# Windowed attention and a gated two-layer product on one core: w_out's load, batch 0's last copies and the global rows' store in other places

## The chip, the cores and the metric

The kernel runs on one core of one Trainium2 chip. The metric is device time in microseconds (us) of the whole program, from three runs; besides these, one execution was recorded by the hardware profiler. Engines: PE (TensorE), DVE (VectorE), ACT (ScalarE), POOL (GpSimd) and SP, which only issues transfers. POOL issues transfers too; those that change the type (from float32 to bfloat16) all go through POOL's queue (q0, "software_dynamic"), SP's through q1 ("hardware_dynamic").

## The reference

Attention with a window of 32 to each side and 8 global tokens that see and are seen by all, for 8 batches, 8 heads, 576 tokens, 64 dimensions; then a product with `w_in`, a Snake activation and a product with `w_out`:

```python
scores = scale * np.matmul(q, k.transpose(0, 1, 3, 2))
mask = np.abs(pos[:, None] - pos[None, :]) <= window
mask = mask | is_global[:, None] | is_global[None, :]
attn = softmax(np.where(mask, scores, -1e9))        # written out in the reference
x = np.matmul(attn, v).transpose(0, 2, 1, 3).reshape(B * S, H * D)   # 4608 x 512
h = x @ w_in                                        # 4608 x 2048
g = h + np.sin(alpha * h) ** 2 / (alpha + 1e-09)
out = g @ w_out                                     # 4608 x 512, float32
```

## The kernel before

**Stages.** The program is one hand-written order; each engine works off its instructions in the order in which they are written. `phase_a(b, b_moe)` is the attention of batch `b`, with the second product (`gemm2`) of an earlier batch put between its steps; `gemm1(b)` is `x @ w_in` and the activation. The sequence is attention 0, then for each b: gemm1(b), attention(b + 1). Heads go in four pairs `hp`. In a pair: `scores` (PE), exponential to `E` (ACT), mask (DVE), `denominators` (PE, with a matrix of ones), logarithm and inverse exponential (ACT), `numerators` (PE, E with the values VX), product with the inverse into `xT` (DVE). LC keeps the logarithms in SBUF for a later test; they get there by small SP transfers.

**gemm1** runs over 16 groups `nt` of 128 columns of `w_in`. Three PSUM tiles (zn, zr, zd) rotate: PE fills one, ACT takes the sine of it (`sb`), ACT or DVE squares it (`s`), DVE writes `H2` (`H` in the trace) and so frees the tile. **gemm2** is a generator over blocks of 128 tokens, 16 matmuls each into one of two tiles zo, then ACT copies the block to `osb` (three buffers) and SP stores it. `fill(n)` takes its next n matmuls; the tables FIRST, SECOND, NEAR, MIDST, PER_GROUP, GROUP_LATE and GROUP_LAST say how many at which place. Two batches make nine blocks; for the last two, five are left for batch 7.

**Transfers.** For each batch, POOL casts k, q and v to DRAM (`kd`, `qd`, `vd`); SP transposes kd and qd into SBUF (`kt`, `qt`, `turn_qk`), and DVE copies from there into KX and QX (`place`); SP loads vd into VX (`load_v`). Batch 0 has a way of its own: its tokens are loaded directly, transposed by PE, and copied from PSUM by ACT (into KD) and DVE (into QX); the second half of the heads (pairs 2 and 3) is `second_half`. w_in comes in four casts, the last two behind the wait `pace`, which is a copy of one element of kt by POOL to the tile `seen`, so that POOL's queue stands until kt has landed. The global tokens' values are gathered by SP from v into a part of H2 (`gather(v, gv)`), cast by POOL into VGb, and loaded by SP into VX (`load_vg`).

**Global rows.** The output rows of global tokens are computed apart (64 extra columns in batch 7's gemm1, `gemm2_globals` after everything else) and stored by an indirect transfer from POOL (the scatter) over the rows that were stored before. At the end `judge` and `judge_sums` test whether the fast path's assumptions hold; a branch on `verdict` goes to `general_path` if they don't, which it doesn't here.

Of the kernel before, what the change touches and what calls it, by code (L numbers as in the profile page):

```python
# [249 lines left out]
def kernel(  # L250
# [66 lines left out]
    seen = main.tile([1, 1], DT.bfloat16, name="seen")  # L317
# [21 lines left out]
    def cast_v(b):  # L339

        cast[b, "vd"] = dramp.tile([S, H, D], DT.bfloat16, name="vd")
        nc.gpsimd.dma_start(out=cast[b, "vd"][:], in_=v[b].rearrange("h s d -> s h d"))

    def turn_qk(b):

# [435 lines left out]
    def attention_first(beside):  # L781


        b = 0
        kx, qx, VXb = KD, QX[0], VD
        xT = xpool.tile([P, CT, SG], DT.bfloat16, name="xT")
        xTs[b] = xT
        Es, Rs, begun = {}, {}, set()
        ring = tc.alloc_tile_pool(name="ringp", bufs=2, space=PSUM)
        pair = {}  # L790

        def scores(hp, g):
# [12 lines left out]
            nc.vector.tensor_tensor(  # L805
                out=Eg, in0=Eg, in1=MASK[:, 4 * g : 4 * g + 4, :].rearrange("p i c -> p (i c)"),
                op=ALU.mult,
            )

        def nd(hp, key):  # L810


            t = (zn, zd)[key] if hp < NHP - 1 else (pair["zr"] if key else zd)
            return t[:].rearrange("p k (x c) -> p k x c", x=2)

        def products(hp, gs, keys=(0, 1)):


            E = Es[hp][:].rearrange("p i (x c) -> p i x c", x=2)
            for g in gs:  # L820
                for key in keys:
                    out_t = nd(hp, key)
                    for i in range(4 * g, 4 * g + 4):
                        s0 = begin(i)
                        a, z = max(s0, 0), min(s0 + 60, QLEN)
                        if z <= CUT + 4:
                            parts = [(0, a, z)]
                        elif a >= CUT:
                            parts = [(1, a, z)]
                        elif i % 2:  # L830
                            parts = [(0, a, CUT + 4), (1, CUT + 4, z)]
                        else:
                            parts = [(0, a, CUT), (1, CUT, z)]
                        for half, a, z in parts:
                            bank = (hp, key, half)
                            nc.tensor.matmul(
                                out=out_t[:, half, :, a - half * CUT : z - half * CUT],
                                lhsT=OB[:] if key else VXb[:, hp, i, :],
                                rhs=E[:, i, :, a - s0 : z - s0],
                                start=bank not in begun, stop=True, skip_group_check=True,  # L840
                            )
# [12 lines left out]
        def normalise(hp):  # L854
            nc.vector.tensor_tensor(
                out=xT[:, hp, 0:S].rearrange("p (k m c) -> p k m c", k=4, c=KT), in0=body(hp, 0),
                in1=Rs[hp][:], op=ALU.mult,
            )

        def idle(hp):  # L860
            if hp > 1:
                warm(zo[0], 1)

        for hp in range(NHP):
            Es[hp] = pairp.tile([P, NT12, WCOL], DT.bfloat16, name="E")
            for g in range(2):
                scores(hp, g)
                idle(hp)
            if hp:
                products(hp - 1, range(3), (1,))  # L870
            scores(hp, 2)
            idle(hp)
            if hp:
                products(hp - 1, range(3), (0,))
            if hp:
                inverse(hp - 1)
                sums(hp - 1, 1)
# [12 lines left out]
        sums(last, 0)  # L890
        normalise(last)

        beside(NHP)
        after.release()


    def attention(b, beside):
# [208 lines left out]
    def gemm1(b):  # L1106
# [23 lines left out]
        for nt in range(NT):  # L1130
# [33 lines left out]
        hr.release()  # L1164


    def gemm2(b):
        lo, hi = (0, 4) if b % 2 == 0 else (4, 9)
        for blk in range(lo, hi):
            ops = zo[(blk + b // 2) % 2]  # L1170
            for nt in range(NT):
                nc.tensor.matmul(  # L1172
                    out=ops[:], lhsT=H2[:, nt, blk * P : (blk + 1) * P], rhs=w_out[:, nt, :],
                    start=(nt == 0), stop=(nt == NT - 1),
                )
                yield True
            osb = osbp.tile([P, DM], DT.float32, name="osb")
            if b == B - 1 and blk == hi - 1:
                for e, copy in enumerate((nc.scalar.copy, nc.vector.tensor_copy)):
                    copy(out=osb[:, e * DM // 2 : (e + 1) * DM // 2], in_=ops[:, e * DM // 2 : (e + 1) * DM // 2])  # L1180
            else:
                nc.scalar.copy(out=osb[:], in_=ops[:])  # L1182

            c = blk * P
            while c < (blk + 1) * P:
                z = min((c // QTR + 1) * QTR, (blk + 1) * P)
                run, u = c // QTR, c % QTR
                t0 = (b // 2) * 2 * S + (run // 2) * HALF + run % 2 + 2 * u
                nc.sync.dma_start(
                    out=out[t0 : t0 + 2 * (z - c) - 1 : 2, :], in_=osb[c - blk * P : z - blk * P, :]  # L1190
                )
                c = z

    def gemm2_globals():

# [43 lines left out]
    def pace(src):  # L1239

        nc.gpsimd.tensor_copy(out=seen[:], in_=src)  # L1241

    def phase_a(b_att, b_moe):
        def beside(at):

            if b_moe is None:
                if at == 0:
                    second_half()
                    turn_qk(1)
                    pace(turned[1][1][0:1, 0:1])  # L1250
                    load_w_in((2, 3))
                    cast_v(1)
                    load_w_out()
                    gather(v, gv)
                if at == 2:
                    load_v(1)
# [24 lines left out]

    phase_a(0, None)
    for b in range(B):
        if b == 1:
            pace(turned[2][0][0:1, 0:1])
            cast_v(2)
# [8 lines left out]
        if b + 1 < B:  # L1295
# [19 lines left out]
    with tc.If(sure < P):  # L1315
        general_path(tc, q, k, v, global_idx, out, w_in, w_out, alphaT, recipT)


# [28 lines left out]
```

## Time and profile before

| | |
|---|---|
| median of 3 runs | 382.67 us (382.43 to 382.87) |
| the profiled execution | 384.38 us, span 382.7 us, mean granted PE clock 0.97 |
| busy: PE, weight loads, DVE, ACT, POOL | 323.6, 206.1, 275.5, 288.9, 55.1 us |
| q0, POOL's queue | 18.52 MB, 39.9% of 16 DMA engines |
| q1, SP's queue | 23.97 MB, 30.2% |

Shares are of the span. A row of a timeline is start, duration, engine, line, operation, what is written <- what is read, count, and in brackets the idle time of the engine before it with what ended that. A row with "SPq" or "POOLq" is the issuing of a transfer and not its landing. "xN" rows are merged: the duration is from the first to the last of N.

### The profile page before, as it was taken

The page shows a single profiled execution, that of the slowest core. Times are in us where ns is not written, and L with a number is a line of the kernel's source. Part 1 is how long each engine was busy: PE and PEld are TensorE (multiplying, and loading weights), DVE is VectorE, ACT ScalarE, POOL GpSimd, SP SyncE. Part 2 cuts the span into 40 slices and gives each one's busy share as a digit, 9 for nine tenths or more (in the row PEclk, how much of TensorE's full clock was granted, in tenths as well). Part 3 has the DMA queues.
Part 4 walks back from the last instruction along what each step waited for, and adds up shares of the span by engine and source line. Part 5 has one row for each costly group of instructions (what it writes and reads, how often), then busy time and mean ns, then how long its engine had stood idle before and what let it go on. Part 6 is the DMA issues. An engine that isn't in the chain of part 4 may idle for free. (4 is left out here: it accounts for less than half of the span.)

```text
span 382.7 us, 10443 instructions
## 1 busy us (share of the span) xinstructions
PE 323.6 (85%) x4222; PEld 206.1 (54%) x4280; DVE 275.5 (72%) x539; ACT 288.9 (75%) x425; POOL 55.1 (14%) x78
## 2 busy tenths in 40 slices
PE   2678753699988998899899989998998998899990
PEld 2566532356645664566556655665466655554440
DVE  6966897156969687967796788778877885889400
ACT  7879794278877888879887987898888886889110
POOL 7941730014004000400030002100000000000001
PEclk9999995599999999999999999999999999999996
DMA  7999999179994991395849693977232020002221
GB/s 121 117 162 170 184 207 224 27 153 153 203 196 80 208 183 30 69 189 100 149 81 163 119 153 86 146 155 123 59 93 51 0 58 32 3 0 83 64 75 49
DMA packets 91393, 43.23 MB, mean 113 GB/s; under 512 B 76394, under 2 KB 85994, under 8 KB 90890
## 3 DMA queue, kind: packets, MB, share of 16 engines
q0 software_dynamic: 44208, 18.52, 39.9%
q1 hardware_dynamic: 47130, 23.97, 30.2%
q8 instruction: 35, 0.57, 0.6%
q14 instruction: 20, 0.16, 0.1%
HBM read 41.97 MB, written 21.95 MB: 167 GB/s over the span
## 5 line engine op out<-in xcount | busy, mean ns | idle before, releaser
L1172 PE MATMUL zo<-w_out,H 128*128 128x512 bf16 x518 | 137.5, 382 | 4.6 <-issue 3.6
L1124 PEld LDWEIGHTS <-w_in 128*128 128x128 bf16 x1024 | 99.2, 98 | 53.0 <-issue 18.7
L1172 PEld LDWEIGHTS <-H 128*128 128x128 bf16 x576 | 51.0, 98 | 45.3 <-issue 0.7
L938 ACT ACTIVATE E<-ring 128x720 bf16<-128x720 f32 x56 | 43.3, 773 | 28.8 <-PE ring L929 28.8
L1124 PE MATMUL zn<-xT,w_in 128*128 128x288 bf16 (+1 forms) x384 | 57.0, 287 | 6.1 <-DVE H L1160 4.1
L1124 PE MATMUL zr<-xT,w_in 128*128 128x288 bf16 x320 | 47.7, 287 | 3.3 <-DVE H L1160 2.9
L1124 PE MATMUL zd<-xT,w_in 128*128 128x288 bf16 x320 | 46.3, 287 | 1.9 <-DMA w_in<-in_moe_w_in_dram 1.3
L1160 DVE SCALAR_TENSOR_TENSOR H<-s,recipT,zn 128x576 bf16<-128x576 bf16 (+1 forms) x48 | 39.4, 822 | 10.7 <-ACT s L1157 7.3
L1154 ACT ACTIVATE sb<-zn,alphaT 128x576 bf16<-128x576 f32 (+1 forms) x48 | 35.7, 743 | 14.6 <-PE zn L1124 13.5
L1157 ACT ACTIVATE s<-sb 128x576 bf16<-128x576 bf16 (+1 forms) x62 | 42.7, 689 | 2.0
L1159 DVE TENSOR_TENSOR s<-sb 128x576 bf16<-128x576 bf16 (+1 forms) x66 | 30.9, 468 | 14.2 <-ACT sb L1154 13.1
L939 DVE TENSOR_TENSOR E<-E,MASKT 128x720 bf16<-128x720 bf16 x56 | 29.2, 529 | 11.6 <-ACT E L938 11.1
L1160 DVE SCALAR_TENSOR_TENSOR H<-s,recipT,zd 128x576 bf16<-128x576 bf16 (+1 forms) x40 | 32.9, 822 | 6.4 <-ACT s L1157 4.3
L1160 DVE SCALAR_TENSOR_TENSOR H<-s,recipT,zr 128x576 bf16<-128x576 bf16 (+1 forms) x40 | 32.9, 822 | 5.9 <-ACT s L1157 3.4
L1154 ACT ACTIVATE sb<-zd,alphaT 128x576 bf16<-128x576 f32 (+1 forms) x40 | 29.6, 739 | 5.9 <-PE zd L1124 5.9
L1154 ACT ACTIVATE sb<-zr,alphaT 128x576 bf16<-128x576 f32 (+1 forms) x40 | 29.6, 741 | 3.5 <-PE zr L1124 3.4
L1182 ACT COPY osb<-zo 128x512 f32<-128x512 f32 x35 | 20.4, 582 | 14.2 <-PE zo L1172 14.1
L778 ACT ACTIVATE R<-L,shift 128x576 f32<-128x576 f32 x32 | 24.8, 774 | 0.6
L985 DVE TENSOR_TENSOR xT<-zn,R 128x576 bf16<-128x576 f32 x21 | 15.8, 754 | 8.8 <-PE zn L967 6.0
L1241 POOL COPY seen<-xT 1x1 bf16<-1x1 bf16 x4 | 1.9, 480 | 134.7 <-DVE GN L755 134.7
L1208 POOL DMA_INDIRECT out_dram<-osb,grow x1 | 1.0, 979 | 135.7 <-SPq L1315 135.7
L929 PEld LDWEIGHTS <-KX 64*64 64x64 bf16 x448 | 9.0, 111 | 20.9 <-issue 19.2
(169 smaller groups left out, 373.5 us busy)
## 6 DMA issues: line engine op xcount, KB each, us to landing
kd<-in_k_dram POOLq DMA_DIRECT2D x7, 576.0 KB, 6.5
qd<-in_q_dram POOLq DMA_DIRECT2D x7, 576.0 KB, 10.1
vd<-in_v_dram POOLq DMA_DIRECT2D x7, 576.0 KB, 15.4
VX<-vd SPq DMA_DIRECT2D x16, 168.0 KB
w_in<-in_moe_w_in_dram POOLq DMA_DIRECT2D x4, 512.0 KB, 5.8
w_out<-in_moe_w_out_dram POOLq DMA_DIRECT2D x4, 512.0 KB, 16.4
out_dram<-osb SPq DMA_DIRECT2D x8, 256.0 KB
VD<-vd SPq DMA_DIRECT2D x12, 168.0 KB
```

What stands on the lines that cost most here:

```text
L778: nc.scalar.activation(out=R[:], in_=L[:], func=AF.Exp, scale=-1.0, bias=shift[:, 0:1])
L929: nc.tensor.matmul(out=zs[half * D : (half + 1) * D, t, 0 : G3 * WCOL].rearrange("p (m x c) -> p m x c", x=2, c=60)[:, m % G3, :, c0:c1], ...
L938: nc.scalar.activation(out=Eg, in_=zs[:, :, 0 : G3 * WCOL], func=AF.Exp, scale=scale)
L939: nc.vector.tensor_tensor(out=Eg, in0=Eg, in1=MASKT[:, None, G3 * g : G3 * (g + 1), :].rearrange("p o m c -> p o (m c)").to_broadcast([P, ...
L985: nc.vector.tensor_tensor(out=xT[:, hp, 0:S].rearrange("p (k m c) -> p k m c", k=4, c=KT), in0=tokens(nd(hp, 0)), in1=Rs[hp][:], op=ALU.mult,)
L1124: nc.tensor.matmul(out=h_part, lhsT=w_in[:, c, nt * P : (nt + 1) * P], rhs=xT[:, c, lo:hi], start=(c == 0), stop=(c == CT - 1), skip_group ...
L1154: nc.scalar.activation(out=sb[:, 0:W], in_=h, func=AF.Sin, scale=alphaT[:, nt : nt + 1])
L1157: nc.scalar.activation(out=s2[:, 0:W], in_=sb[:, 0:W], func=AF.Square)
L1159: nc.vector.tensor_tensor(out=s2[:, 0:W], in0=sb[:, 0:W], in1=sb[:, 0:W], op=ALU.mult)
L1160: nc.vector.scalar_tensor_tensor(out=H2[:, nt, r0 : r0 + W], in0=s2[:, 0:W], scalar=recipT[:, nt : nt + 1], in1=h, op0=ALU.mult, op1=ALU.add,)
L1172: nc.tensor.matmul(out=ops[:], lhsT=H2[:, nt, blk * P : (blk + 1) * P], rhs=w_out[:, nt, :], start=(nt == 0), stop=(nt == NT - 1),)
L1182: nc.scalar.copy(out=osb[:], in_=ops[:])
```

## The change

Five things.

1. **w_out and the order of POOL's transfers.** `load_w_out` moves from attention 0 to gemm1(0), group 10, behind `load_vg(1)` and a new `pace` on VX, so it is issued when all of batch 1's values and global values have landed. The `pace` on kt ahead of w_in's second half goes, so w_in and vd follow batch 1's kd and qd at once. `seen` has 128 rows now.
2. **Batch 0's `second_half`** moves from behind pair 0 to pair 1, behind its three exponentials.
3. **NEAR.** `fill(NEAR)` stands ahead of `numerators(last - 1)` instead of behind it, in batches 1 to 7.
4. **The last batch.** GROUP_LAST takes 16 matmuls of gemm2(6) instead of 4. Behind gemm1(7) come the rest of gemm2(6), then `gemm2_globals` and its scatter, and only then gemm2(7), the last five blocks. So that those blocks store the right global rows of batch 7 over the scatter's, `put_globals` copies the eight global columns of H2 on POOL to their tokens' columns; the column numbers are computed by `load_columns` (seven DVE instructions of one row and eight register loads on POOL), written ahead of gemm1(2). `judge_sums` comes behind the globals.
5. **The end.** The last block is computed, copied (by ACT alone) and stored in two halves of 256 columns, and the branch's blocks are laid out the other way round.

POOL's order around w_out, before. `kd`, `qd`, `vd` are the casts of batches 1 (first) and 2, KX_94 and QX_96 batch 1's keys and queries, whose global columns POOL fills:

```order
L335 DMA kd<-in_k_dram 32x9216
L335 DMA qd<-in_q_dram 32x9216
L1241 COPY seen<-kt 1x1
L430 DMA w_in<-in_moe_w_in_dram 128x4x512 x2
L342 DMA vd<-in_v_dram 4608x1x64
L436 DMA w_out<-in_moe_w_out_dram 128x4x512 x4
L1260 COPY MASKT<-MASK 64x720 x2
L719 COPY VGb<-H_97 64x512
L377 COPY KX_94<-kTg 128x48x8
L380 COPY QX_96<-qTg 128x4x7x4 x2
L335 DMA kd<-in_k_dram 32x9216
L335 DMA qd<-in_q_dram 32x9216
```

And now, in the same place of POOL's queue (VX_93 is batch 1's values):

```order
L336 DMA kd<-in_k_dram 32x9216
L336 DMA qd<-in_q_dram 32x9216
L435 DMA w_in<-in_moe_w_in_dram 128x4x512 x2
L343 DMA vd<-in_v_dram 4608x1x64
L1292 COPY MASKT<-MASK 64x720 x2
L724 COPY VGb<-H_97 64x512
L382 COPY KX_94<-kTg 128x48x8
L385 COPY QX_96<-qTg 128x4x7x4 x2
L347 COPY seen<-VX_93 56x1
L441 DMA w_out<-in_moe_w_out_dram 128x4x512 x4
L336 DMA kd<-in_k_dram 32x9216
L336 DMA qd<-in_q_dram 32x9216
```

The wait on kt is gone ahead of w_in; a wait on VX stands ahead of w_out, and batch 2's casts stand behind both. SP's own order there is the same as before.

ACT's order in batch 0's attention, before, from the first pair's exponentials (`E<-ring`) on; `KD<-zn` are the eight copies of `second_half`:

```order
L804 ACTIVATE E<-ring 128x480 [waits PE_49] x2
L627 COPY KD<-zn 64x24x12 x8
L804 ACTIVATE E<-ring 128x480 [waits PE_49] x3
L771 ACTIVATE L<-zd 128x576 [waits DVE_49]
L778 ACTIVATE R<-L,shift 128x576 [waits Activation_49]
```

And now:

```order
L809 ACTIVATE E<-ring 128x480 [waits PE_49] x5
L632 COPY KD<-zn 64x24x12 x8
L776 ACTIVATE L<-zd 128x576 [waits DVE_49]
L783 ACTIVATE R<-L,shift 128x576 [waits Activation_49]
```

The copies moved behind the second pair's three exponentials, and stand right ahead of the first pair's logarithm `L`.

SP's last stores, before, with what each waits for (Activation and DVE are the copies of the block, DMAHW and DMASW earlier transfers):

```order
L1189 DMA out_dram<-osb 64x512 [waits DMAHW6_49,Activation_49]
L1189 DMA out_dram<-osb 64x512 [waits DMAHW7_49]
L1314 TENSOR_LOAD verdict [waits DVE_49]
L1314 ISA x2
L1189 DMA out_dram<-osb 80x512 [waits DMAHW0_49,Activation_49]
...
L1189 DMA out_dram<-osb 16x512 [waits DMAHW5_49]
L1189 DMA out_dram<-osb 128x512 [waits DMAHW6_49,DVE_49]
```

And now:

```order
L1228 DMA out_dram<-osb 64x512 [waits DMAHW6_49,DMASW4_49,Activation_49]
L1228 DMA out_dram<-osb 64x512 [waits DMAHW7_49]
L1228 DMA out_dram<-osb 80x512 [waits DMAHW0_49,Activation_49]
...
L1352 TENSOR_LOAD verdict [waits DVE_49]
L1352 ISA x2
...
L1228 DMA out_dram<-osb 16x512 [waits DMAHW5_49]
L1228 DMA out_dram<-osb 128x256 [waits DMAHW6_49,Activation_49]
L1228 DMA out_dram<-osb 128x256 [waits DMAHW7_49,Activation_49]
```

The first store of the last five blocks now waits for the scatter too (DMASW4), and the last block's store is two.

The diff, cut:

```diff
+    def pace(src):
+        nc.gpsimd.tensor_copy(out=seen[0 : src.shape[0]], in_=src)
...
             scores(hp, 2)
+            if hp == 1:
+                second_half()
             idle(hp)
...
         inverse(last - 1)
+        fill(NEAR)
         numerators(last - 1)
-        fill(NEAR)
         denominators(last)
...
                 load_vg(1)
+                pace(VX[1][D : D + NK, 0, 0, 0:1])
+                load_w_out()
...
+    def put_globals():
+        for j, c in enumerate(columns_of):
+            g = 2 * S + j * B + B - 1
+            nc.gpsimd.tensor_copy(out=H2[:, :, bass.ds(c, 1)], in_=H2[:, :, g : g + 1])
...
-    GROUP_LAST = (0, 0, 2) + 2 * (0, 0, 0, 1) + 5 * (0,)
+    GROUP_LAST = (0, 0, 3) + 13 * (1,)
...
                 if at == 0:
-                    second_half()
                     turn_qk(1)
-                    pace(turned[1][1][0:1, 0:1])
                     load_w_in((2, 3))
                     cast_v(1)
-                    load_w_out()
                     gather(v, gv)
...
+        if b == 2:
+            load_columns()
...
-    waiting.append(gemm2(B - 1))
+    put_globals()
     square_x(B - 1, 0)
     square_x(B - 1, 1)
-    for c in range(CT):
+    square_w(0)
+    fill(NT)
+    square_w(1)
+    fill(4 * NT)
+    gemm2_globals()
+    judge_sums()
+    waiting.append(gemm2(B - 1))
+    for c in (2, 3):
         square_w(c)
         fill(NT)
-        if c == 1:
-            judge_sums()
     judge()
     fill(2 * NT * NT)
-    gemm2_globals()
     mctx.close()
...
-    with tc.If(sure < P):
+    with tc.If(sure < P, preferred_fallthrough_block=False):
```

More of the change, by code (lines that the diff above doesn't have):

```diff
@@ L316 @@
     VG0 = main.tile([NG * B, D], DT.bfloat16, name="VG0")
-    seen = main.tile([1, 1], DT.bfloat16, name="seen")
+    seen = main.tile([P, 1], DT.bfloat16, name="seen")
+    gcol = main.tile([1, NG], DT.int32, name="gcol")
     girow = main.tile([1, NG], DT.int64, name="girow")
@@ L1164, in gemm1, with load_columns @@
         hr.release()
+    columns_of = []
+    def load_columns():
+        ci = normp.tile([1, 4, NG], DT.int32, name="ci")
+        cf = normp.tile([1, 4, NG], DT.float32, name="cf")
+        nc.vector.tensor_copy(out=ci[:, 0], in_=gi32[:, 0::2])
+        nc.vector.tensor_scalar(out=ci[:, 1], in0=ci[:, 0], scalar1=1, scalar2=None, op0=ALU.bitwise_and)
+        nc.vector.tensor_copy(out=cf[:, 0:2], in_=ci[:, 0:2])
+        nc.vector.tensor_scalar(
+            out=cf[:, 2], in0=cf[:, 0], scalar1=float(HALF), scalar2=float(QTR), op0=ALU.is_ge, op1=ALU.mult
+        )
+        nc.vector.scalar_tensor_tensor(
+            out=cf[:, 3], in0=cf[:, 0], scalar=0.5, in1=cf[:, 2], op0=ALU.mult, op1=ALU.add
+        )
+        nc.vector.scalar_tensor_tensor(
+            out=cf[:, 3], in0=cf[:, 1], scalar=float(QTR) - 0.5, in1=cf[:, 3], op0=ALU.mult, op1=ALU.add
+        )
+        nc.vector.tensor_scalar(out=gcol[:], in0=cf[:, 3], scalar1=float(S), scalar2=None, op0=ALU.add)
+        for j in range(NG):
+            columns_of.append(nc.gpsimd.value_load(gcol[0:1, j : j + 1], min_val=S, max_val=2 * S - 1))
+    def put_globals():
+        for j, c in enumerate(columns_of):
+            g = 2 * S + j * B + B - 1
+            nc.gpsimd.tensor_copy(out=H2[:, :, bass.ds(c, 1)], in_=H2[:, :, g : g + 1])
     def gemm2(b):
@@ L1170, in gemm2, with store @@
             ops = zo[(blk + b // 2) % 2]
[L1171 to L1176, printed above, removed]
-            osb = osbp.tile([P, DM], DT.float32, name="osb")
[L1178 to L1192, printed above, removed]
+            osb = osbp.tile([P, DM], DT.float32, name="osb")
+            parts = 2 if (b, blk) == (B - 1, hi - 1) else 1
+            for part in range(parts):
+                cols = slice(part * DM // parts, (part + 1) * DM // parts)
+                for nt in range(NT):
+                    nc.tensor.matmul(
+                        out=ops[:, cols], lhsT=H2[:, nt, blk * P : (blk + 1) * P], rhs=w_out[:, nt, cols],
+                        start=(nt == 0), stop=(nt == NT - 1), skip_group_check=True,
+                    )
+                    yield True
+                nc.scalar.copy(out=osb[:, cols], in_=ops[:, cols])
+                store(b, blk, osb, cols)
+    def store(b, blk, osb, cols):
+        c = blk * P
+        while c < (blk + 1) * P:
+            z = min((c // QTR + 1) * QTR, (blk + 1) * P)
+            run, u = c // QTR, c % QTR
+            t0 = (b // 2) * 2 * S + (run // 2) * HALF + run % 2 + 2 * u
+            nc.sync.dma_start(
+                out=out[t0 : t0 + 2 * (z - c) - 1 : 2, cols], in_=osb[c - blk * P : z - blk * P, cols]
+            )
+            c = z
     def gemm2_globals():
@@ L1237, in places_at @@
         return PLACES[slice(*share.get(at, (0, 0)))]
-    def pace(src):
-        nc.gpsimd.tensor_copy(out=seen[:], in_=src)
     def phase_a(b_att, b_moe):
```

## The prediction

> **What bounds the kernel now.** I read the page first, then the waits, then PE's timeline wherever PE stands still, then POOL, SP and the DMA queues around those places, and the tail last. The page's DMA line (40 slices of 9.6 us) shows the first third saturated, so a transfer that is put later there pushes what stands behind it:
>
> ```profile
> DMA  7999999179994991395849693977232020002221
> ```
>
> PE's timeline (start, duration, what, and in brackets the idle time before it) shows the longest stop, in batch 1's attention. PE waits 4.82 + 2.39 = 7.2 us for batch 1's values VX, and only then comes the first product with w_out:
>
> ```profile
> 62.56 0.51 PE L929 MATMUL ring<-QX,KX 64*64 64x88 bf16 x13 [0.38 <-DVE QX L357]
> 67.89 0.28 PE L967 MATMUL zn<-E,VX 56*64 56x88 bf16 x2 [4.82 <-DMA VX<-VGb]
> 70.56 0.78 PE L967 MATMUL zn<-E,VX 56*64 56x88 bf16 x26 [2.39 <-DMA VX<-VGb]
> 71.27 0.61 PE L1172 MATMUL zo<-w_out,H 128*128 128x512 bf16 x1
> ```
>
> POOL and SP, which issue the transfers, show why:
>
> ```profile
> 23.69 0.53 POOL L335 DMA_DIRECT2D qd<-in_q_dram  x1
> 36.65 0.18 POOL L1241 COPY seen<-kt 1x1 bf16<-1x1 bf16 x1 [12.44 <-DMA kt<-kd]
> 36.88 1.54 POOL L430 DMA_DIRECT2D w_in<-in_moe_w_in_dram  x2
> 38.41 2.26 POOL L342 DMA_DIRECT2D vd<-in_v_dram  x1
> 40.12 3.53 POOL L436 DMA_DIRECT2D w_out<-in_moe_w_out_dram  x4
> 49.86 0.72 POOL L719 CAST VGb<-H 64x512 bf16<-64x512 f32 x1 [4.58 <-DMA LC<-L]
> 83.97 0.18 POOL L1241 COPY seen<-qt 1x1 bf16<-1x1 bf16 x1 [30.65 <-DMA qt<-qd]
> ```
>
> ```profile
> 34.39 2.32 SPq L348 DMA_TRANSPOSE qt<-qd  x1
> 36.90 6.76 SPq L508 DMA_DIRECT2D H<-in_v_dram  x8
> 51.60 1.63 SPq L418 DMA_DIRECT2D VX<-vd  x4
> 54.51 1.35 SPq L422 DMA_DIRECT2D VX<-VGb  x2
> 75.18 2.21 SPq L348 DMA_TRANSPOSE kt<-kd  x1
> ```
>
> VX is issued at 51.6 to 55.9 but lands at 70.5, because four casts of w_out (2 MB) and then batch 2's keys and queries (1.2 MB) use the same engines. The same rows show a second chain: batch 2's transposes start at 75.18, `seen` sees them done at 83.97, and only then POOL casts batch 2's values and batch 3. That chain is late again at 111.68, where DVE waits for batch 3's keys (first row), and PE for DVE (second):
>
> ```profile
> 111.68 0.92 DVE L364 COPY KX<-kt 64x1152 bf16<-64x1152 bf16 x2 [3.29 <-DMA kt<-kd]
> 113.22 0.80 PE L967 MATMUL zd<-E,ones 56*64 56x88 bf16 x28 [0.81 <-DVE E L939]
> ```
>
> So whatever PE gains at 63 to 71 is kept at 113 only as far as the transfers move too, plus 0.8 us.
>
> **Transfers, part by part.** Two edits meet. The wait for kt goes, so w_in's second half and vd follow qd at once instead of at 36.9; and w_out goes behind a new wait for all of VX, with batch 2's casts behind it. DMA queue rows of four stretches of 2 us (34 to 36, 40 to 42, 46 to 48, 52 to 54: packets, MB, share) give the rates of transposes, w_in, vd and w_out:
>
> ```profile
> q1 hardware_dynamic: 1981, 0.50, 110.9%
> q0 software_dynamic: 381, 0.39, 118.5%
> q0 software_dynamic: 2225, 0.28, 222.1%
> q0 software_dynamic: 415, 0.41, 123.2%
> ```
>
> Transposes: 1.2 MB at 0.25 MB/us, 4.7 us. w_in: 1.0 MB at 0.195, 5.3 us. vd: 4608 packets at 1112 per us, 4.1 us. Together 14.1 us; if the engines keep these rates when shared, and qd is drained by about 31.5 (estimate, from the transposes having the engines to themselves at 34), all are done at 45.6. The transposes then end with the rest, instead of at about 39 (estimate: alone, with a slow start). SP stands in order: its issue of qt ended at 36.7, some 2.3 us before the data, and so ends at about 43.3 now; the eight gathers of the global values behind it (6.76 us) end at 50.1. They land some 1.5 us later, POOL casts VGb until 52.3, SP issues VX<-VGb at about 53 to 54.5. These are the old times. What is new is that VX has the engines alone: 0.8 MB at 0.2 to 0.25 MB/us is 3.5 us, and I let V land at 58 instead of 70.5. The bounds are 51 (transposes undisturbed: gathers at 36.9 as now, VX issued when vd is in) and 70.5.
>
> From there: w_out starts at 59.2; w_out and batch 2's casts are 3.2 MB at 0.205, 15.5 us, to 74.7. w_out comes in quarters of 2.5 us, from about 63, and PE takes the first at 64.1 (71.27 less 7.2) and then four matmuls for each quarter, with scores and products between them: no stop, just. But batch 2's keys land at 73, when SP would have wanted them at 68. With 22.5 us from V to the end of the transposes, `seen` comes at 80.5 and not 83.97: **-3.5 us**, and batch 3's keys and so PE's 113.22 move by that, though PE could have been 7.2 earlier. Each us that V lands later is a us lost.
>
> Ahead of that stand edits that this chain covers. w_in's wait goes (row below: 1.3 us gained). The last heads' copies go behind the second pair's exponentials: ACT copied for 3.22 us first, now it does two exponentials, idles for the third's scores, then copies, which frees zn, for which PE waits from then on:
>
> ```profile
> PE zd L1124 <- DMA w_in<-in_moe_w_in_dram: 1.3, 1, 1.3
> 16.68 3.22 ACT L627 COPY KD<-zn 64x288 bf16<-64x288 bf16 x8
> 21.73 1.31 PE L836 MATMUL zn<-E,VD 128*128 128x88 bf16 x14 [0.64 <-DMA VD<-in_v_dram]
> ```
>
> zn's products come at about 22.7 instead of 21.73: 1.0 us lost (0 to 1.5). Both matter only if V comes so early that PE sets the pace; they cancel within 0.3, and I enter nothing.
>
> **The other terms.** `load_columns` puts seven one-row instructions on DVE ahead of batch 2's first group, at the duration of the first row (0.16, some 0.2 from start to start): 1.4 us, of which DVE's idle 0.62 (second row) covers part. DVE frees the bank that PE takes next, so **+0.8** (0 to 1.0). POOL's eight register loads stand where POOL has nothing to do for 30 us. NEAR: three matmuls now stand ahead of the numerators, which in two batches waited as in the third row: **-0.6** (0 to -0.7).
>
> ```profile
> 358.92 0.16 DVE L1094 TENSOR_TENSOR cm<-cm,xm 128x1 f32<-128x1 f32 x1
> 128.97 0.46 DVE L1159 TENSOR_TENSOR s<-sb 128x576 bf16<-128x576 bf16 x1 [0.62 <-ACT sb L1154]
> 162.22 0.50 PE L967 MATMUL zn<-E,VX 56*64 56x88 bf16 x28 [0.34 <-DVE GN L755]
> ```
>
> The tail, PE first, then what ends the run; the last row is from the DMA issues (last figure: us from issue to landing):
>
> ```profile
> 324.54 1.25 PE L1124 MATMUL zd<-xT,w_in 128*128 128x288 bf16 x8
> 343.21 13.98 PE L1172 MATMUL zo<-w_out,H 128*128 128x512 bf16 x62
> 372.06 1.94 PE L1200 MATMUL zd<-w_out,H 128*64 128x256 bf16 x32
> 369.74 3.68 SPq L1189 DMA_DIRECT2D out_dram<-osb  x2
> 374.08 0.37 ACT L1207 COPY osb<-zd 64x256 f32<-64x256 f32 x1 [1.50 <-PE zd L1200]
> 375.73 0.04 POOLq L1208
> 376.59 0.98 POOL L1208 DMA_INDIRECT out_dram<-osb,grow  x1 [135.74 <-SPq L1315]
> out_dram<-osb,grow POOLq DMA_INDIRECT x1, 4.4
> ```
>
> Twelve more matmuls (0.2255 us each, 13.98/62: 2.7 us) go from the tail into the last gemm1, whose groups take 1.27 us ((18.67 - 4 x 0.2255)/14) for 8 matmuls of 288 and 352 columns. Free if PE waits there anyway, worth nothing if it doesn't: **-1.5** (0 to -2.7). Halving the last block costs a little for 32 short matmuls instead of 16: **+0.2**. The end: PE's last matmul ends at 374.0, the span at 382.7, 8.7 us later; the scatter, issued at 376.59, lands at 381.0, and 1.7 us follow. Now a copy (0.45), SP's issue (0.4), a store's landing (373.42 to 375.73 at most: 2.3) and the same 1.7 make 4.8: **-3.9** (-2 to -5). [...] The eight column copies on POOL must be done before the last five blocks; 36 matmuls (8.1 us) and the globals' 1.94 lie ahead of those on PE. At the 0.5 us of POOL's small copies they take 4 us: nothing, and up to 3 us if they took 1.6 each. The scatter is now waited for by SP's next store; three output buffers cover that.
>
> Sum: -3.5 + 0.8 - 0.6 - 1.5 + 0.2 - 3.9 = -8.5. The profiled execution took 384.38 (span 382.7 and 1.7 around it) and would take 375.9; it lies 1.7 above the median of the runs, 382.67, from which I forecast 374.2.
>
> **The rivals.** *V lands by 53.* The transposes are not slowed by w_in and vd. PE is then 7.2 us earlier and keeps it: -12.2, 370.5. For it: `seen` waited until 36.65 for kt, whose 0.6 MB are 2.4 us at the rate above, so much of a transpose's time isn't transfer. Against: two streams at 118% and 111% of the engines can't both run at full rate.
>
> *The clock falls again.* Windows of 1 us (span, PE, weight loads, DVE, ACT, POOL, granted clock, DMA share, GB/s) show the clock fall at 59, when PE had had little to do since 55, and stay at half until 76, some 5 us after PE had work again:
>
> ```profile
> 59.00:60.00 1.00, 0.54 (x27) 0.54 (x30) 1.00 (x2) 0.41 (x1) 0.00 (x0) 0.64 1.05 222
> 75.00:76.00 1.00, 1.00 (x43) 0.90 (x42) 0.00 (x0) 0.33 (x1) 0.00 (x0) 0.50 0.09 21
> 76.00:77.00 1.00, 0.76 (x17) 0.51 (x9) 0.52 (x1) 1.00 (x2) 0.00 (x0) 0.83 0.55 107
> ```
>
> In my forecast PE stands still for 0.8 + 3.7 = 4.5 us ahead of 113.22; 5 us at half clock afterwards cost 2.5: -6.0, 376.7. [...]
>
> *V lands at 62 to 66.* The transposes end late or the gathers land slowly: the front is +0.5 to +4.5, 378.2 to 382.2.
>
> *V lands as late as now (slower).* The one mechanism that turns the sign: everything from w_out to batch 3 now stands behind V. The place is POOL's `seen<-VX`. At 70.5 the transposes of batch 2 end at 93, 9 us later than now: +4.0, 386.7. It decides from V at 66.5 (front +5.0, which the other five terms just pay). For it: VX<-VGb took 15 us from issue to landing. Against: that was beside w_out.
>
> **How the numbers follow.** Forecast 0.36; V by 53, 0.22; clock 0.18; V at 62 to 66, 0.11; V as late as now, 0.11; 0.02 for the kernel ending where it did. 0.2% is 0.8 us, about what a measurement of this kernel can tell from no change. Faster: 0.36 + 0.22 + 0.18 + 0.10 = 0.86; same 0.02; slower 0.12. The range leaves out the slower rival and the far ends: 368.5 (V early, and the tail's better bounds in part) to 381.
>
> **What would show it.** `seen<-VX` ending near 58 on POOL, PE's wait ahead of the numerators at 63 gone, and no wait for w_out over 1 us; batch 2's transposes done near 80.5; DVE's wait for batch 3's keys longer than 3.29 by about 3.7; PE's end to the span's end 4.8 us. Wrong if V lands after 62 or before 53, if DVE waits for qt ahead of batch 1, or if PE waits for POOL ahead of the last five blocks.

## The result, and the profile after

The changed kernel takes 387.41 us (median of 4 runs, 385.94 to 388.07) against 382.75 before (4 runs, 382.43 to 382.87): ratio 1.0118, 95% interval 1.0086 to 1.0150. It is slower, by 1.2%, and the forecast was faster. The profiled execution took 387.9 us, span 386.2, 3.5 more than that of before. (Later comparisons were made on other chips, where the kernel before took 380 to 382 us; each is given as a ratio to it there, and a ratio leaves out slow runs, those over 1.5% above the fastest run of their kernel.)

The page's PEclk and DMA lines, 40 slices of 9.65 us. The clock now dips twice. The DMA engines, full from 10 to 67 us before, are half idle from 48 to 68, while the gathers, VGb and VX are waited for one after the other:

```profile
PEclk9999995599996999999999999999999999999998
DMA  7999955997997795159396946598314111000231
```

PE's timeline at the three places that were shown of before. The stop of 7.2 us for VX is gone. In its place stand a stop for POOL's copy of the global queries, one for w_out, and at 120.02 one of 6.6 us where it was 0.81:

```profile
58.58 0.35 PE L936 MATMUL ring<-QX,KX 64*64 64x88 bf16 x14 [3.74 <-POOL QX L385]
...
70.72 0.58 PE L1214 MATMUL zo<-w_out,H 128*128 128x512 bf16 x1 [3.92 <-DMA w_out<-in_moe_w_out_dram]
...
120.02 0.96 PE L974 MATMUL zd<-E,ones 56*64 56x88 bf16 x28 [6.61 <-DVE E L946]
```

POOL and SP, which issue the transfers (before: VGb cast 49.86, batch 2's casts 52.22, `seen<-qt` 83.97; qt's issue ended 36.7):

```profile
56.50 0.61 POOL L724 CAST VGb<-H 64x512 bf16<-64x512 f32 x1 [26.16 <-DMA H<-in_v_dram]
...
57.84 0.69 POOL L385 COPY QX<-qTg 128x112 bf16<-128x112 bf16 x2
64.02 0.21 POOL L347 COPY seen<-VX 56x1 bf16<-56x1 bf16 x1 [5.49 <-DMA VX<-VGb]
64.47 3.00 POOL L441 DMA_DIRECT2D w_out<-in_moe_w_out_dram  x4 [0.24 <-issue]
67.43 0.55 POOL L336 DMA_DIRECT2D kd<-in_k_dram  x1
...
90.22 0.18 POOL L347 COPY seen<-qt 1x1 bf16<-1x1 bf16 x1 [21.73 <-DMA qt<-qd]
```

```profile
29.67 10.19 SPq L353 DMA_TRANSPOSE kt<-kd  x1
39.96 7.04 SPq L353 DMA_TRANSPOSE qt<-qd  x1
47.20 7.77 SPq L513 DMA_DIRECT2D H<-in_v_dram  x8
...
64.52 9.99 SPq L778 DMA_DIRECT2D LC<-L  x2
82.04 3.33 SPq L353 DMA_TRANSPOSE kt<-kd  x1
```

The two transposes of batch 1 hold SP for 10.19 and 7.04 us instead of 4.68 and 2.32. The reader should see the staircase: qt ends at 47.0, the gathers behind it at 55.0, VGb's cast at 57.1, POOL's QX behind that at 58.5 (PE's 3.74 us), VX is seen at 64.0, w_out is issued behind it, batch 2's casts at 67.4 behind w_out, and its transposes are seen at 90.2, 6.25 us later than before.

DVE's wait for batch 3's keys (3.29 us before) makes PE's 6.61. Two windows of 1 us (span, PE, weight loads, DVE, ACT, POOL, granted clock, DMA share, GB/s) show the clock falling towards half inside that stop and back at full at 124; the windows between have it at 0.50, four us of them with PE at work again:

```profile
118.48 0.92 DVE L369 COPY KX<-kt 64x1152 bf16<-64x1152 bf16 x2 [9.09 <-DMA kt<-kd]
```

```profile
117.00:118.00 1.00, 0.00 (x0) 0.00 (x0) 0.00 (x0) 0.00 (x0) 0.00 (x0) 0.58 0.05 5
...
124.00:125.00 1.00, 0.90 (x4) 0.29 (x3) 0.95 (x3) 0.74 (x2) 0.00 (x0) 1.00 0.00 0
```

From PE's 120.02 (before 113.22) the difference between the two kernels goes on like this: +6.8; +8.0 when the clock is back; +8.64 at the end of batch 2's gemm1 (`load_columns`); +7.12 at batch 7's gemm1 (NEAR); +7.90 at its end; +6.33 at PE's last matmul; +3.5 at the end of the span. So the end paid as meant, and the front cost more than the end brought.

### The profile page after: what moved, and what is told of

It reads as the page before. It is cut to its first block, busy times and chain, and to the rows that moved or that the text cites. A ratio compares the mean times of both kernels' runs of the same rounds, so it can differ in the third digit from the quotient of the medians.

```text
span 386.2 us, 10526 instructions
## 1 busy us (share of the span) xinstructions
PE 324.1 (84%) x4238; PEld 209.1 (54%) x4296; DVE 277.9 (72%) x545; ACT 288.5 (75%) x426; POOL 58.8 (15%) x86
## 4 chain that ended last, share of the span: by engine, by line
PE 39%; DVE 17%; ACT 14%; DMA 12%; SPq 7%; issue 6%; POOL 4%; DVEq 0%; ACTq 0%; POOLq 0%
PE zo L1214 19%; PE zn L1131 7%; ACT sb L1163 7%; DVE H L1169 6%; SPq L353 4%; DMA kt<-kd 4%; PE zr L1131 4%; DMA w_out<-in_moe_w_out_dram 3%; PE zd L1131 3%; DVE s L1168 2%; DVE E L946 2%; PE ring L936 2%; ACT s L1166 2%; DMA kd<-in_k_dram 2%; DMA VD<-in_v_dram 2%
## 5 line engine op out<-in xcount | busy, mean ns | idle before, releaser
L1214 PE MATMUL zo<-w_out,H 128*128 128x512 bf16 (+1 forms) x534 | 139.6, 378 | 10.8 <-DMA w_out<-in_moe_w_out_dram 5.3
L1214 PEld LDWEIGHTS <-H 128*128 128x128 bf16 x592 | 53.3, 98 | 51.2 <-issue 8.2
L1219 ACT COPY osb<-zo 128x512 f32<-128x512 f32 (+1 forms) x37 | 21.1, 569 | 16.4 <-PE zo L1214 10.3
L1203 POOL COPY H<-H 128x16 bf16 x8 | 5.0, 629 | 105.4 <-DVE H L1169 104.9
L936 PE MATMUL ring<-QX,KX 64*64 64x120 bf16 (+2 forms) x448 | 12.6, 226 | 9.8 <-ACT E L945 3.9
```

Source lines behind the costliest of these rows:

```text
L936: nc.tensor.matmul(out=zs[half * D : (half + 1) * D, t, 0 : G3 * WCOL].rearrange("p (m x c) -> p m x c", x=2, c=60)[:, m % G3, :, c0:c1], ...
L1214: nc.tensor.matmul(out=ops[:, cols], lhsT=H2[:, nt, blk * P : (blk + 1) * P], rhs=w_out[:, nt, cols], start=(nt == 0), stop=(nt == NT - 1) ...
L1219: nc.scalar.copy(out=osb[:, cols], in_=ops[:, cols])
```

## The experiments

Two readings of the front stood against each other. A (the transfers' own speed): without the wait for kt, the casts slow the transposes and V comes late; w_out behind V is harmless. B (the order in the queue): w_out behind V puts batch 2's casts behind V and w_out, whatever the transposes do. The first four kernels undo or do one part alone.

**e1, the wait for kt put back into the changed kernel.**

```diff
                     turn_qk(1)
+                    pace(turned[1][1][0:1, 0:1])
                     load_w_in((2, 3))
```

> The changed kernel with one line added: POOL waits for batch 1's transposed keys kt again before it casts w_in's second half and v. Theory A (the lost wait on kt is what costs: casts and transposes share the DMA engines packet by packet, SP's transposes, the gathers behind them and so VGb come 11 us later): SP ends issuing qt's transposes near 37 again instead of 47, VGb is cast near 48 to 50 instead of 56.5, V lands at 54 to 57 instead of 64, batch 2's transposes are seen at 80 to 83 instead of 90.2, and the time is 376 to 380. Theory B (w_out behind V costs by itself, since batch 2's casts stand behind it whatever the transposes do): V lands at 60 or later, transposes seen after 86, time 383 to 387.

384.92 us (4 runs), ratio 1.0109 (1.0069 to 1.0148): as slow against before as the changed kernel. SP and POOL in its trace:

```profile
34.35 3.23 SPq L353 DMA_TRANSPOSE qt<-qd  x1
```

```profile
60.59 0.48 POOL L347 COPY seen<-VX 56x1 bf16<-56x1 bf16 x1 [7.90 <-DMA VX<-VGb]
...
64.11 0.55 POOL L336 DMA_DIRECT2D kd<-in_k_dram  x1
```

The transposes are quick again and V is seen at 60.6, ten us sooner than it landed before. Yet batch 2's casts are issued at 64.1 and its transposes seen at 86.8, and PE stops for 7.6 us. A is not the whole.

**e2, the kernel before with w_out alone behind V.**

```diff
-                    load_w_out()            # attention 0
...
                 load_vg(1)
+                pace(VX[1][D : D + NK, 0, 0, 0:1])
+                load_w_out()
```

> The kernel before with w_out's load alone moved behind the wait for batch 1's V; the wait on kt stays, and nothing else is changed. Theory A: V at 54 to 57 instead of 70.5, batch 2's transposes seen at 80 to 83 instead of 84, DVE's wait for batch 3's keys about as long as in the kernel before, time 380 to 382.5. Theory B: the move costs by itself, transposes seen at 86 to 90, time 385 to 389.

389.31 us (4 runs), ratio 1.0229 (1.0192 to 1.0266). V seen 60.6, transposes 86.9, PE's stop 7.7 us: e1 again, without what the end gains. B is right for this edit. Not all of the price is the stop itself. The clock falls in it and is at 0.50 from 114 to 123, though PE is at work again from 117.5 (two windows, columns as above):

```profile
114.00:115.00 1.00, 0.00 (x0) 0.00 (x0) 0.00 (x0) 0.00 (x0) 0.00 (x0) 0.50 1.80 44
122.00:123.00 1.00, 1.00 (x4) 0.30 (x2) 0.97 (x3) 0.20 (x1) 0.00 (x0) 0.50 0.00 0
```

PE begins batch 2's denominators 4.3 us later than before (117.48 for 113.22), and takes 16.06 us from there to batch 2's gemm1, for 13.05: 3.0 us more. In e1 it is the same, with the clock at 0.50 from 114 to 124: 15.20 us, where a kernel without the long stop (e4 below) takes 12.63.

**e3, the kernel before without the wait for kt.**

```diff
                     turn_qk(1)
-                    pace(turned[1][1][0:1, 0:1])
                     load_w_in((2, 3))
```

> The kernel before with the wait on kt alone taken out; w_out stays where it was, ahead of batch 1's V. Theory A: SP ends issuing qt's transposes near 47, VGb is cast near 56, V lands at 71 to 76, time 384 to 389. Theory B: the casts only start earlier, time 381 to 383.

389.76 us (4 runs), ratio 1.0221 (1.0178 to 1.0265). So this edit alone costs as much: A is right for it, and without the half clock (it is at 1.00 from 82 to 122 us): PE begins batch 2's denominators at 119.14, 5.9 us later than before, after a stop of only 1.5 us, and takes the usual 13.04 us to gemm1. SP's rows:

```profile
30.22 10.18 SPq L348 DMA_TRANSPOSE kt<-kd  x1
40.51 7.96 SPq L348 DMA_TRANSPOSE qt<-qd  x1
48.66 11.60 SPq L508 DMA_DIRECT2D H<-in_v_dram  x8
```

The three issues take 29.7 us instead of 13.8; DVE waits 9.2 us for qt, POOL casts VGb at 66.9. Each edit alone costs 2.2 to 2.3%; the changed kernel has both, and `second_half`'s move, and pays 2.4% for them (1.0118 less e4's 0.9878, below). The prices do not add up: either edit, and both, lead to batch 2's transposes seen at 87 to 90.

**e4, the changed kernel with the front of before** (w_out, the wait for kt and `second_half` in their old places; NEAR, the global rows and the end as changed).

```diff
-            if hp == 1:
-                second_half()
...
-                pace(VX[1][D : D + NK, 0, 0, 0:1])
-                load_w_out()
...
                 if at == 0:
+                    second_half()
                     turn_qk(1)
+                    pace(turned[1][1][0:1, 0:1])
                     load_w_in((2, 3))
                     cast_v(1)
+                    load_w_out()
```

> The changed kernel with batch 0's and batch 1's part as before: the wait on kt, w_out's place and second_half's place are those of the kernel before; NEAR, the last batch and the end are changed. Both theories: the front costs what the changed kernel lost and the rest gains: PE's first product behind batch 3's keys near 113.2 as before, then 1.5 us from NEAR, 1.9 from the last gemm1, 2.8 from the end, less 0.7 for load_columns and 1.1 for the last block: 378.3 (377 to 380). If it is above 382, the tail's gains seen in the changed kernel's trace are not what they seem.

378.14 us (10 runs), ratio 0.9878 (0.9832 to 0.9924), which is -4.7 us; the forecast's terms for these parts sum to -5.0. The whole loss lies in the front.

**e5 and e6, batch 2's casts ahead of the wait for V and of w_out**; e6 has the wait for kt too.

```diff
                 load_vg(1)
+                cast_qk(2)
                 pace(VX[1][D : D + NK, 0, 0, 0:1])
                 load_w_out()
...
             if b == 0:
-                cast_qk(2)
+                pass
```

> The changed kernel with one thing moved: POOL issues the casts of batch 2's keys and queries ahead of the wait for VX and of w_out, not behind both. Theory C (the price of the change is the place of those casts in POOL's queue: batch 2's transposes are seen 22.7 us after the casts are issued, and batch 3's keys follow): casts at about 58.6 and not 67.4, transposes seen at 81 to 85 and not 90.2, PE's stop ahead of batch 2's denominators under 2 us and not 6.6: 379 to 382.5. Theory D (the bytes have to pass before about 113 whatever the order; what is put ahead holds up the other): V lands at 67 or later, PE waits longer for w_out, and the time stays at 385 to 389.

> The same, with the wait for kt put back too, so that the transposes of batch 1 run without w_in's and vd's casts beside them; of the front's edits only w_out behind V and second_half are left, with batch 2's casts ahead of w_out. Theory C: casts issued at about 52.5, transposes of batch 2 seen at 75 to 81, no stop ahead of batch 2's denominators, 376 to 379 (the kernel with the old front took 378.1). Theory D: V beside the casts lands at 64 or later, w_out's first quarter at 70 or later, PE waits for it with its clock at half: 380 to 385.

e5: 388.54 us (4 runs), ratio 1.0234 (1.0137 to 1.0331). e6: 383.03 us (10 runs), ratio 1.0091 (1.0036 to 1.0146). Both times are D's. Theory C, that the place of those casts in POOL's queue is the price, falls. In e5 V is seen at 69.4 and the transposes at 91.6. In e6 the casts are issued at 50.4 and the transposes still seen at 87.4. SP and PE say why:

```profile
62.28 13.36 SPq L778 DMA_DIRECT2D LC<-L  x2
75.74 4.99 SPq L353 DMA_TRANSPOSE kt<-kd  x1
80.84 2.68 SPq L353 DMA_TRANSPOSE qt<-qd  x1
```

```profile
71.86 1.44 PE L1215 MATMUL zo<-w_out,H 128*128 128x512 bf16 x3 [6.30 <-DMA w_out<-in_moe_w_out_dram]
```

V now shares the engines with the casts and is seen at 65.3; w_out follows, PE waits 6.3 us for it, so ACT's logarithm L comes late, and SP's store LC<-L, which waits for L, holds the transposes until 75.7. Then they run beside w_out: 4.99 and 2.68 us. The same gate stood in the kernel before, where PE waited for V instead:

```profile
61.37 13.71 SPq L773 DMA_DIRECT2D LC<-L  x2
```

**e7, a swap.** The front of e4, with batch 2's casts at 40 us, where w_out was, and w_out where they were, with no wait.

```diff
                     cast_v(1)
-                    load_w_out()
+                    cast_qk(2)
                     gather(v, gv)
...
             if b == 0:
-                cast_qk(2)
+                load_w_out()
```

> The old front (wait for kt, no wait for VX, second_half in its old place; the end's edits kept; 378.1 so far) with two steps of POOL swapped: batch 2's casts (1.2 MB) at 40 us where w_out (2 MB) was, and w_out at 52 us where they were. Ahead of V stand 0.8 MB less. Theory C: V lands some 3 to 4 us sooner than 70, batch 2's transposes are seen well before 84, DVE's wait of 4.1 us for batch 3's keys goes, 374 to 377.5. Theory D: w_out lands 6 us later than now, PE waits for it where it waited for V, and nothing is gained: 378 to 383.

375.58 us (10 runs), ratio 0.9903 (0.9858 to 0.9948). Its interval overlaps e4's, so the medians don't tell the two apart; their traces, one execution of each, differ. SP and PE:

```profile
62.29 9.18 SPq L778 DMA_DIRECT2D LC<-L  x2
71.57 2.33 SPq L353 DMA_TRANSPOSE kt<-kd  x1
```

```profile
66.00 0.28 PE L972 MATMUL zn<-E,VX 56*64 56x88 bf16 x2 [1.92 <-DMA VX<-VGb]
```

V is there at 66, w_out makes PE wait nowhere for 0.7 us or more, SP is free at 71.5, and PE reaches batch 2's denominators at 108.8 instead of 112.5 in e4. So w_out may come later at no loss that shows; what costs is to hold it until V has landed (e2, e6).

**e8, half of w_out behind the casts** (front of e4; quarters 2 and 3 behind `cast_qk(2)`).

```diff
-                    load_w_out()
+                    load_w_out((0, 1))
...
                 cast_qk(2)
+                load_w_out((2, 3))
```

> The old front (378.1 so far) with only w_out's second half (1 MB) behind batch 2's casts, its first half where it was, and no wait for VX. Theory C: V 3 to 5 us sooner, batch 2's transposes seen 1 to 4 us sooner than 84, 375 to 377.5. Theory D: the second half runs beside batch 2's transposes and slows these as w_in and vd slowed those of batch 1 (10.2 and 7.0 us of issue for 4 and 2.4), so that they are seen later than 84: 379 to 383.

379.70 us (10 runs), ratio 0.9972 (0.9924 to 1.0019): no gain over e4, as D had it, but not for D's reason. V still lands at 70.9 and the transposes are seen at 84.3, issued in 2.2 and 2.8 us. The wait for VX hardly moved, with 1 MB less of w_out ahead and 1 MB more behind; which transfers held it stays open.

**e9, w_in alone ahead of the wait for kt** (front of e4).

```diff
-                    pace(turned[1][1][0:1, 0:1])
                     load_w_in((2, 3))
+                    pace(turned[1][1][0:1, 0:1])
```

> The old front (378.1 so far), with only w_in's second half ahead of the wait for kt; vd stays behind it. Which cast slows the transposes of batch 1? vd has 4608 packets of 128 B, w_in some 1000 of 1 KB, and the two rings were seen to serve packets one for one. Theory P (packets): w_in costs the transposes 1000 turns at most, 1 to 5 us of issue in all (kt and qt 6.3 us together now, 17.2 with w_in and vd), the gathers end at 45 to 49, and what V loses there w_in's earlier end pays in part: 377.5 to 380.5. Theory Q (any cast beside a transpose stalls it): kt and qt take 14 us or more, the gathers end after 52, V lands after 72: 382 to 387.

378.23 us (12 runs), ratio 0.9960 (0.9924 to 0.9995). The time lies in P's range, but on another chip than e4's 378.14; the issue is nearly Q's: 13.3 us, not 7 to 11. SP's rows, and the two queues from 36 to 38 us (packets, MB, share):

```profile
29.78 9.95 SPq L353 DMA_TRANSPOSE kt<-kd  x1
39.83 3.30 SPq L353 DMA_TRANSPOSE qt<-qd  x1
```

```profile
q0 software_dynamic: 153, 0.16, 49.8%
q1 hardware_dynamic: 147, 0.04, 18.6%
```

153 packets of w_in against 147 of the transposes: w_in's packets are four times as large (about 1 KB), and for each of them the transposes get one of 256 B (0.50 MB in 1981 packets from 34 to 36 us before). Both are slow here, w_in at 0.08 MB/us where it had 0.195 almost alone (before, 40 to 42 us); as the packets of both take only 68% of the engines' time, the packet counts alone don't explain it, and no run here does. Against e4 nothing is gained: 0.996 for 0.988, with intervals that meet at 0.9924. Part of what the gathers lose comes back, since w_out, now behind the longer wait, is issued 5 us later, and batch 2's transposes are seen at 80.2. How much of the time is the one and how much the other stays open.

**e10, `second_half` behind the second pair's exponentials in e7.**

```diff
             scores(hp, 2)
+            if hp == 1:
+                second_half()
```

> The swapped kernel (375.6 so far; batch 2's casts ahead of w_out, wait for kt) with the last heads' copies behind the second pair's exponentials, as in the changed kernel. Theory C (covered): PE's later products, 1.3 us, are eaten by its waits for w_in (1.5 us) and VX (1.9 us): 375.2 to 376.2. Theory D (uncovered): w_in's and VX's waits hide no more than half, and the gemm of batch 0 starts 1 to 2 us later: 376.4 to 377.6.

376.33 us (6 runs), ratio 0.9880 (0.9837 to 0.9923): e7's ratio lies within this interval, and the median between C's range and D's, so the time decides nothing. In the trace batch 0's gemm starts 1.7 us later than in e7 (33.41 against 31.72), which D had named; but PE's wait for VX falls from 1.92 to 0.6 us, and batch 1's gemm1 starts only 0.25 later (78.05 against 77.80), which is C.

**e11, `load_columns` inside DVE's wait, and the two halves of the last block in two banks** (on e7).

```diff
+            if b_att == 2 and at == -1:
+                load_columns()
...
-        if b == 2:
-            load_columns()
...
+                if part:
+                    ops = zo[(blk + b // 2 + 1) % 2]
```

> The swapped kernel (375.6 so far) with load_columns' seven DVE instructions put where DVE waits 3.5 us for batch 3's keys anyway, and the second half of the last block in the other bank, so that it doesn't wait 0.5 us for ACT's copy of the first half. Theory C: PE loses neither the 0.65 us ahead of batch 2's first group nor the 0.5 us of the tail: 374.2 to 375.0. Theory D: the time goes to other waits: 375.4 to 376.0.

374.56 us (6 runs), ratio 0.9854 (0.9807 to 0.9902). DVE's wait behind the seven instructions is 2.67 instead of 3.50, and the keys are copied no later; the tail's 0.51 us is gone too. The time is C's, though the interval doesn't exclude D:

```profile
106.79 0.92 DVE L369 COPY KX<-kt 64x1152 bf16<-64x1152 bf16 x2 [2.67 <-DMA kt<-kd]
```

**e12, batch 2's transposes ahead of the store LC<-L** (on e7).

```diff
-            if b_moe == 0 and at == 2:
+            if b_moe == 0 and at == 1:
                 turn_qk(2)
```

> The swapped kernel (375.6 so far) with the transposes of batch 2 issued one head pair earlier, ahead of the store LC<-L, behind which they stood on SP until 71.6 (in the kernel before until 75.1). Theory E (they stand behind PE's progress): they start at about 64 to 66, are seen at 74 to 78 and not 80.3, DVE's wait of 3.5 us for batch 3's keys and PE's of 1.0 go: 374 to 375. Theory F (they then run beside w_out's casts and VX, 10 + 7 us of issue, and VX and w_out land later): seen at 80 or later, PE waits for w_out: 376 to 380.

374.00 us (5 runs, 373.05 to 374.67), ratio 0.9811 (0.9768 to 0.9854): the lowest median, though not to be told from e11's, and the whole interval lies below before. Both theories hold in part; SP's rows:

```profile
63.46 7.27 SPq L353 DMA_TRANSPOSE kt<-kd  x1
70.84 5.08 SPq L353 DMA_TRANSPOSE qt<-qd  x1
```

The transposes start at 63.5 instead of 71.6 and, beside w_out, take 12.4 us instead of 4.9; they are seen at 78.0, 2.4 us sooner than in e7.

The stages of ten of the kernels together (us; the gathers' end is that of SP's issue; "keys" is DVE's copy of batch 3's keys, the stop PE's ahead of batch 2's denominators):

| kernel | gathers end | batch 2: cast, transposed from, seen | keys | stop | ratio |
|---|---|---|---|---|---|
| before | 43.7 | 52.2, 75.2, 84.0 | 111.7 | 0.8 | 1 |
| after | 55.0 | 67.4, 82.0, 90.2 | 118.5 | 6.6 | 1.012 |
| e1 | 44.5 | 64.1, 78.5, 86.8 | 116.4 | 7.6 | 1.011 |
| e2 | 44.7 | 64.1, 78.4, 86.9 | 115.9 | 7.7 | 1.023 |
| e3 | 60.3 | 68.9, 81.1, 90.1 | 117.6 | 1.5 | 1.022 |
| e4 | 43.5 | 51.9, 74.6, 84.0 | 110.9 | 1.6 | 0.988 |
| e6 | 43.0 | 50.4, 75.7, 87.4 | 115.1 | 1.9 | 1.009 |
| e7 | 44.3 | 40.7, 71.6, 80.3 | 107.3 | 1.0 | 0.990 |
| e9 | 50.3 | 58.3, 71.2, 80.2 | 107.4 | 1.8 | 0.996 |
| e12 | 44.7 | 41.1, 63.5, 78.0 | 106.1 | under 0.7 | 0.981 |

From "seen" to "keys" it is 27 to 30 us in every row, so what moves "seen" moves the keys. The ratio doesn't follow in proportion: in e1 and e2 the half clock behind the long stop comes on top, and e7 and e9, with "seen" some 3.7 us sooner than e4, have no lower ratio than e4.

## Why the prediction was wrong

**The step that failed is the front: "seen comes at 80.5 and not 83.97: -3.5 us".** It came at 90.22. Of the 9.7 us between, 6.0 are V (64.0 and not 58) and 3.7 the way from V to there (26.2 and not 22.5).

**V at 58.** The rates were taken from stretches in which each queue had the engines nearly to itself, and summed (14.1 us, to 45.6). In six of the seven stretches of 2 us from 34 to 48 us, the engines served the two queues about packet for packet (224 of q1 to 221 of q0 in the first, 872 to 806 in the last); the queue rows from 42 to 44 us:

```profile
q1 hardware_dynamic: 764, 0.20, 87.3%
q0 software_dynamic: 764, 0.10, 81.6%
```

764 packets of each, 1528 in all, where the transposes alone had 1981 (before, 34 to 36 us): they get less than two fifths of those, 0.10 MB/us instead of 0.25. In e9 it is 153 packets to 147 from 36 to 38 us. (From 44 to 46 us it is 1703 casts' packets to 343; what held the transposes there no run shows.) So the transposes' 4608 packets were through at about 49.5 and not 45.6, an estimate from the queue rows up to 50 us: the sum was 4 us too small. The steps behind came later by as much or more: qt's issue ended at 47.0, not 43.3, and the gathers at 55.0, not 50.1. From the end of VX's issue (60.6) to `seen<-VX` it was 3.4 us, as forecast. The rival "V at 62 to 66" is where V came; its 378.2 to 382.2 was too low for the reasons that follow. The rival "V by 53" needed transposes that casts don't slow; they were slowed, and even in e1, where they weren't (though vd was cast later there), V was seen at 60.6.

**V + 22.5.** The wait for V, w_out's issue and its start put the casts' issue at V + 3.4, and their first data were in at V + 18.0, not V + 15: SP waited for them.

```profile
SPq L778 <- ACT L L776: 12.7, 2, 8.9
...
SPq L353 <- DMA kd<-in_k_dram: 7.5, 1, 7.5
```

**"Each us that V lands later is a us lost", and the turning point at V = 66.5.** With V at 64 the forecast's own terms gave 380.2. Against the measured 387.4 that is 7.2 short: 3.7 from V to `seen`; 0.55 more at PE (6.8 for 6.25); 1.2 by the half clock; 0.9 by the halved last block; 1.1 by the last store; less 1.5 that NEAR, the last gemm1 and `load_columns` did better than forecast; and 1.2 because before's profiled execution lay 1.7 above its median and the changed kernel's 0.5. And the turning point was set too late: in e1 V is there at 60.6, with every other term in place, and the kernel is still slower than before.

**What PE was to gain.** The 7.2 us at VX were to be PE's. They went to two waits that the forecast had as none: 3.74 for QX, because POOL's copies of the global keys and queries stand behind VGb's cast, and 3.92 for w_out, which took 1.42 more at 79.47. SP reached its store of L at 74.5 instead of 75.1: of 7.2 us, 0.6 were left at the place that frees the transposes.

**The slower rival** had the right mechanism (everything from w_out to batch 3 stands behind V, at `seen<-VX`) with the wrong price: it needed V at 66.5, and V at 64, or at 60.6 in e1, was enough.

**The clock rival** was real: the fall at 117 to 124 above, 1.2 us and not 2.5. In e1 and e2, with stops of 7.6 and 7.7 us, it cost 2.6 and 3.0. It came beside the loss and not in place of the gain.

**second_half** was to cost 1.0 (0 to 1.5). PE's products came at 23.03 for 21.73, 1.3 later, but batch 0's gemm 2.25 later. DVE's mask product took 1.52 us instead of 0.41 while POOL copied MASKT. The rows of DVE and POOL:

```profile
28.17 1.52 DVE L810 TENSOR_TENSOR E<-E,MASK 128x480 bf16<-128x480 bf16 x1 [1.56 <-ACT E L809]
```

```profile
28.12 2.21 POOL L1292 COPY MASKT<-MASK 64x720 bf16<-64x720 bf16 x2
```

In e10, where POOL copies MASKT later (at 40.79), the same product took its usual time, and the gemm came 1.7 later than in e7:

```profile
28.42 0.41 DVE L810 TENSOR_TENSOR E<-E,MASK 128x480 bf16<-128x480 bf16 x1 [1.57 <-ACT E L809]
```

What ties the 1.52 us to POOL's copy, no run shows.

**The end was right, a little too large.** Batch 7's first product with w_in starts at 328.35, 7.12 us later than before (321.23), against 8.64 at the end of batch 2's gemm1: I put the 1.5 between, for 0.6 forecast, to NEAR, which no run tried alone. gemm1(7) took 0.8 us more with 12 matmuls (2.7) in it: -1.9 for -1.5. The tail:

```profile
351.11 8.58 PE L1214 MATMUL zo<-w_out,H 128*128 128x512 bf16 x39
353.93 5.46 POOL L1203 COPY H<-H 128x16 bf16 x8 [104.93 <-DVE H L1169]
378.42 1.91 PE L1214 MATMUL zo<-w_out,H 128*128 128x256 bf16 x16 [0.50 <-ACT osb L1219]
```

The eight column copies took 5.5 us for 4 and were hidden. The halved block cost 1.1 for 0.2, worked out from the 1.6 us that PE gained behind gemm1(7) of the 2.7 moved out of it: 0.50 is its wait for ACT's copy of its own first half, in the same bank, which is gone in e11; the rest is not accounted for. From PE's last matmul to the end of the span it was 5.9 us instead of 8.7: -2.8 for -3.9.

```profile
378.40 2.72 SPq L1228 DMA_DIRECT2D out_dram<-osb  x2
```

SP's issue ends at 381.1, and 5.1 us follow, where I had summed 4.0. `load_columns` cost 0.65 for 0.8.

## What to carry to other kernels

A transfer that "can come later" stands in a queue: before moving it behind a wait, list what is behind it in that queue, follow that to the next wait of the busy engine, and give each link its slack; here the casts behind w_out had none. Where two queues run at once, don't add up rates that each had alone: count packets too, for here each queue got about every second one in six of the seven stretches from 34 to 48 us, whatever its packets carried (the casts' about 1 KB from 36 to 38 us, 128 B from 42 to 44). And in this kernel a late transfer was better put behind another transfer (e7, no loss against e4 that shows) than behind a wait for one (e2, 2.3% lost).

## What had not been expected of the hardware

SP's issue of a transpose took longer when casts ran beside it, and what stands behind it on SP began that much later: the gathers at 47.20, where they began at 36.90 before. For batch 1, kt's issue took 3.1 to 4.8 us in the ten kernels with the wait for kt ahead of w_in, and 9.9 to 10.3 in the four with casts beside it (after, e3, e5, e9). qt's took 2.2 to 3.2, against 7.0 to 8.0 in three of these (after, e3, e5); in e9, where w_in was through by then, it took 3.3. Alone the transposes moved 0.25 MB/us (before, 34 to 36 us), more than the casts of w_in and w_out did almost alone (0.195 and 0.205; before, 40 to 42 and 52 to 54 us); beside a cast it was 0.10 (after, 42 to 44 us).
